# Folding v into w_in: the low parts as eight 64-row products that share one round

## The chip, the cores and the metric

One Trainium2 chip, one of its cores. The metric is the device time of one execution in microseconds (us). The matrix engine is called PE here (its weight loads PEld), the vector engine DVE, the scalar engine ACT, GpSimd POOL; SP issues most transfers.

## The reference

Eight batches of eight heads; 576 tokens, head size 64, 32 memory slots per head. The attention is followed by a feed-forward layer.

```python
a = softmax(phi over the 32 slots)                     # (b, h, s, m)
k_m = einsum('bhsm,bhsd->bhmd', a, k)                  # 32 x 64 per head
v_m = einsum('bhsm,bhsd->bhmd', a, v)
attn = softmax(q @ k_m.T / 8)                          # 576 x 32 per head
x = concat over heads of (attn @ v_m)                  # 4608 x 512
h = x @ w_in                                           # 4608 x 2048
out = (h * cos(h)) @ w_out                             # 4608 x 512
```

## The kernel before

`x` is never formed. For each batch the kernel folds `v_m` into `w_in`: for head h the 32 x 64 block of `v_m` times the 64 rows of `w_in` that belong to it gives 32 rows of a table `vw`, 256 rows (8 heads) by 2048 columns for a batch. The first product of the feed-forward layer is then `vw` times the attention weights (`gemm1`, L568), the second one multiplies by `w_out` (`gemm2`, L628). Both have float16 operands in two parts, a high one and a low one (what the float16 rounding left over), as three products: high by high, high by low, low by high.

The main loop runs over 12 groups of 384 tokens and, in a group, over 16 steps f of 128 columns of `h`. A step is `gemm1` (six matmuls of 384 columns into a PSUM tile `hp`), then sine and products on ACT and DVE (`act`, `act_end`: L593, L598, L603, L607, L609, L610), which leave the tile `gp`, and, four steps later (LAG), `gemm2` (nine matmuls of 512 columns into three `acc` tiles). Between them stand the preparation of the next batch (`memory`: maximum and exponential of phi, L304 and L310, the sums `psA` of L256, the turned sums `tpx`, from which `spread_k` fills `km` and `spread_v` fills `vm`; then `attend`: the scores `sc` of L401, their softmax, and `aT`) and its fold.

The fold of a batch goes by quarters q of 512 columns, and in a quarter by halves g of four heads (128 rows of `vw`); half and half stand in one step of the loop, the quarters four steps apart. `fold_psum` writes a half into a PSUM tile `pv`, a whole bank; `split_fold` then makes the high part on ACT (L505) and the low one on DVE (L507). `pv` comes out of a pool of two banks (`ps_s`), which `sc`, `psA`, `tpx` and others share. For the batches 0 and 1 the fold is in float32 (L492). From batch 2 on (`b >= 2`) `v` too has a high part `vp` and a low part `vl`, made in `scales` (L368 to L370), and `w2` holds for each head pair c and head o of it the high part of `w_in` in that head's own 64 partitions and the low part in the 64 partitions of the other. A product of `vp` over all 128 rows is so high by high plus high by low. `vl` is filled in the head's own 64 rows and zero in the others, so that its product over 128 rows is low by high. A product is 32 columns of weights wide and goes to 32 partitions of `pv`; four of them, j = 0 to 3, one for each head, stand side by side. I call four such matmuls of 512 columns, one beside the other, a round.

Up to the middle of the first groups the order is written out by hand (`ORDER`); from the loop on, a scheduler decides the order of each engine's instructions out of the program's order and its own estimate.

Of the kernel before, what the change touches and what calls it, by code (L numbers as in the profile page):

```python
# [20 lines left out]
P = 128  # L21
B, H, S, D, M = 8, 8, 576, 64, 32
# [3 lines left out]
NP = H // 2  # L26
# [47 lines left out]
def attention_then_ffn(ctx: ExitStack, tc: tile.TileContext, phi, phiT, kv, kv_first, qT, w_in, w_out, eye, out):  # L74
    nc = tc.nc
# [8 lines left out]
    def small_ps(name):  # L84
        return ps_s.tile([P, 512], F32, tag="ps_s", name=name)
# [16 lines left out]
    vl = const.tile([P, NP, 2, M], F16, name="vl")  # L102
    nc.vector.memset(vl, 0.0)

    loads, st = {}, {}
# [87 lines left out]
    def to_range(name, pool, tag, e):  # L193
        t = pool.tile([P, 1], F32, tag=tag, name=name)
        nc.vector.reciprocal(out=t, in_=e)
        nc.vector.tensor_scalar(out=t, in0=t, scalar1=2.0 ** 14, scalar2=None, op0=ALU.mult)
        return t
# [62 lines left out]
    def blank(b):  # L260
        st["km", b] = wk.tile([P, NP, 2 * M], F32, tag="km", name=f"km_{b}", bufs=1)
        st["vm", b] = wk.tile([P, NP, 2 * M], F32, tag="vm", name=f"vm_{b}")
        nc.gpsimd.memset(st["km", b], 0.0)
        nc.gpsimd.memset(st["vm", b], 0.0)

    def spread_k(b, tpx):
        tv = tpx[:, 0:HM].rearrange("p (c t m) -> p c t m", t=2, m=M)
        nc.scalar.mul(st["km", b][0:D, :, 0:M], tv[0:D, :, 0], 1.0 / math.sqrt(D))
        nc.scalar.mul(st["km", b][D:P, :, M:2 * M], tv[D:P, :, 1], 1.0 / math.sqrt(D))

    def copier(name):
        return nc.scalar.copy if name in COPY_ACT else nc.vector.tensor_copy

    def spread_v(b, tpx, copy):
        tv = tpx[:, 0:HM].rearrange("p (c t m) -> p c t m", t=2, m=M)
        copy(out=st["vm", b][D:P, :, 0:M], in_=tv[D:P, :, 0])
        copy(out=st["vm", b][0:D, :, M:2 * M], in_=tv[0:D, :, 1])

    def bound(b, X):
        l1 = wk.tile([P, 4], F32, tag="l1", name=f"l1_{b}")  # L280
# [7 lines left out]
    def memory(b):  # L288
# [42 lines left out]
        for g in range(2):  # L331
            nc.tensor.transpose(tpx[:, g * P:(g + 1) * P], X[:, g], ident)
        blank(b)
        spread_k(b, tpx)
        spread_v(b, tpx, nc.vector.tensor_copy)
        yield
        l2 = bound(b, X)
# [12 lines left out]
    def scales(b):  # L350
        E = wk.tile([P, 1], F32, tag="E", name=f"E_{b}", bufs=3)
        nc.vector.tensor_scalar(out=E, in0=st["ev", b], scalar1=st["e", "in"], scalar2=None, op0=ALU.mult)
        cu = wk.tile([P, 1], F32, tag="cu", name=f"cu_{b}", bufs=3)
        nc.vector.tensor_scalar(out=cu, in0=E, scalar1=2.0 ** -27 / (2.0 * math.pi), scalar2=None, op0=ALU.mult)
        st["E", b], st["cu", b] = E, cu
        if b < 2:
            T = wk.tile([P, 1], F32, tag="T", name=f"T_{b}")
            nc.vector.reciprocal(out=T, in_=E)
            nc.vector.tensor_scalar(out=T, in0=T, scalar1=2.0 ** 13, scalar2=None, op0=ALU.mult)
            st["T", b] = T  # L360
        else:

            sv = to_range(f"sv_{b}", wk, "sv", st["ev", b])
            vp = wk.tile([P, NP, 2, M], F16, tag="vp", name=f"vp_{b}", bufs=1)
            for o in range(2):
                here, there = slice(o * D, (o + 1) * D), slice((1 - o) * D, (2 - o) * D)
                vm = st["vm", b][here, :, (1 - o) * M:(2 - o) * M]
                nc.scalar.activation(vp[here, :, o], vm, AF.Copy, scale=sv[here])  # L368
                nc.scalar.activation(vp[there, :, o], vm, AF.Copy, scale=sv[here])
                nc.vector.scalar_tensor_tensor(out=vl[here, :, o], in0=vm, scalar=sv[here], in1=vp[here, :, o],  # L370
                                               op0=ALU.mult, op1=ALU.subtract)
            st["vp", b] = vp
# [114 lines left out]
    def fold_psum(b, q, g):  # L487
        pv = small_ps(f"pv_{b}_{q}_{g}")
        for i in range(2):
            c = 2 * g + i  # L490
            if b < 2:
                nc.tensor.matmul(pv[D * i:D * (i + 1)], lhsT=st["vm", b][:, c],  # L492
                                 rhs=w_in_sb[:, 2 * q:2 * q + 2, c], start=True, stop=True)
        if b >= 2:
            for first in (True, False):
                for j in range(4):
                    c, o = 2 * g + j // 2, 1 - j % 2
                    nc.tensor.matmul(pv[M * j:M * (j + 1)], lhsT=(st["vp", b] if first else vl)[:, c, o],  # L498
                                     rhs=st["w2", q][:, c, o], start=first, stop=not first, skip_group_check=True)
        return pv  # L500

    def split_half(b, vw, g, src, part):
        T = st["T", b] if b < 2 else 2.0 ** -15
        if part == 0:
            nc.scalar.activation(vw[:, 0, g], src, AF.Copy, scale=T)  # L505
        else:
            nc.vector.scalar_tensor_tensor(out=vw[:, 1, g], in0=src, scalar=T, in1=vw[:, 0, g],  # L507
                                           op0=ALU.mult, op1=ALU.subtract)

    def split_fold(b, vw, g, src):  # L510
        for part in range(2):
            split_half(b, vw, g, src, part)

    def fold(b, q, g):
        if g == 0:
            st["vw", b, q] = wk.tile([P, 2, 2, FS], F16, tag="vw", name=f"vw_{b}_{q}", bufs=8)
        split_fold(b, st["vw", b, q], g, fold_psum(b, q, g))

    def fold_first(j, x=slice(0, WS)):
        pv = small_ps(f"pvf_{j}").rearrange("p (g x) -> p g x", g=2)  # L520
# [326 lines left out]
    for v, k in enumerate("kv"):  # L847
# [3 lines left out]
        put(f"X{k}0_1", lambda: norm(0, 1))  # L851
        put(f"tp{k}0", lambda: turn_x(0))
    put("blank0", lambda: blank(0))
    put("km0", lambda: spread_k(0, r["tpk0"]))
    put("vm0", lambda: spread_v(0, r["tpv0"], copier("vm0")))

    def after_memory(b):
        if b:
            for c in range(5):
                put(f"ga{b}_{c}", lambda c=c: gathered(b, c))  # L860
            put("den1", lambda: den_of(1))
            put(f"X{b}_0", lambda: norm(b, 0))
            put(f"X{b}_1", lambda: norm(b, 1))
            put(f"tpx{b}", lambda: turn_x(b))
            put(f"blank{b}", lambda: blank(b))
            put(f"km{b}", lambda: spread_k(b, r[f"tpx{b}"]))
            put(f"vm{b}", lambda: spread_v(b, r[f"tpx{b}"], copier(f"vm{b}")))
        put(f"bound{b}", lambda: set_bound(b))
        put(f"acr{b}", lambda: turn_column(st["l2", b], b))
        put(f"level{b}", lambda: level(b))  # L870
        put(f"att{b}", lambda: do.setdefault(b, attention(b)))
# [39 lines left out]
    for kind, j in blocks:  # L911
# [5 lines left out]
        for w, tag in halves:  # L917
# [10 lines left out]
            if kind == "in":  # L928
                x = slice(0, WS) if w is None else slice(w * P, (w + 1) * P)
# [87 lines left out]
    for b in range(2):  # L1017
        put(f"sc_{b}", lambda b=b: scales(b))
    for g in range(2):
        for part, engine in enumerate(("ACT", "DVE")):  # L1020
            put(f"hi0_{g}_{part}", lambda g=g, part=part: scaled(0, 0, g, st["vf", 0][:, g], part))
        put(f"fo1_{g}", lambda g=g: fold_psum(1, 0, g))
        for part, engine in enumerate(("ACT", "DVE")):
            put(f"hi1_{g}_{part}", lambda g=g, part=part: scaled(1, 0, g, r[f"fo1_{g}"], part))
# [41 lines left out]
    for i in range(NF, 12 * NF):  # L1066
# [21 lines left out]
        for b, q, g in folds.get(i, ()):  # L1088
            if q == g == 0:
                scales(b)  # L1090
            fold(b, q, g)
# [70 lines left out]
```

## Time and profile before

| | us |
|---|---|
| time, median of 3 runs (lowest, highest) | 692.75 (692.67, 693.51) |
| the profiled execution's own time | 693.0 |
| its span, first to last instruction | 691.2 |

Busy time in the span of 691.2 us: PE 680.5, DVE 528.0, ACT 502.9, POOL 36.6, weight loads 360.7. Busy times of PE count each matmul from its start to its modelled end, and these overlap; the distance from the start of one to the start of the next tells more. The chain that ended last is a walk back from the last instruction to what released it; what stands on it is where time can be gained or lost. Verdicts below go by the median.

### The profile page before, as it was taken

What the parts mean: (1) busy time and instruction counts of PE and PEld (TensorE: products, weight loads), DVE (VectorE), ACT (ScalarE), POOL (GpSimd) and SP (SyncE); (2) the same over time, 40 slices, a digit from 0 to 9 for tenths busy, and PEclk for the clock granted to TensorE, in tenths of its full rate; (3) what the DMA queues carried; (4) which work ended last, traced back from release to release, by engine and by line L of the source; (5) the groups of instructions that cost most, each with busy time, mean ns of one, the idle gap of its engine ahead of it and who ended that gap; (6) DMA issues with size and microseconds to landing.
All of it is one profiled execution on the core that took longest, in us unless ns stands there. A gap on an engine that the chain in (4) does not pass through costs nothing.

```text
span 691.2 us, 12016 instructions
## 1 busy us (share of the span) xinstructions
PE 680.5 (98%) x4670; PEld 360.7 (52%) x4670; DVE 528.0 (76%) x1125; ACT 502.9 (73%) x950; POOL 36.6 (5%) x51
## 2 busy tenths in 40 slices
PE   8999999999999999999999999999999999999997
PEld 4545455564544446655454445655445445565553
DVE  6878889999989965798668876599667886566552
ACT  3677878998987866887776965878667875665652
POOL 3433100000001000010000000010000000000000
PEclk9999999999999999999999999999999999999999
DMA  8998906038246100430105300250100100100101
GB/s 300 393 353 328 347 12 176 1 78 271 61 151 153 46 0 25 168 97 1 46 3 172 114 1 2 71 184 34 47 1 1 46 1 1 46 1 1 46 1 46
DMA packets 32585, 66.17 MB, mean 96 GB/s; under 512 B 2192, under 2 KB 12496, under 8 KB 32528
## 3 DMA queue, kind: packets, MB, share of 16 engines
q1 hardware_dynamic: 28208, 57.55, 25.6%
q10 hardware_dynamic: 4320, 7.87, 3.0%
q8 instruction: 36, 0.59, 0.3%
q14 instruction: 21, 0.17, 0.1%
HBM read 51.77 MB, written 9.44 MB: 89 GB/s over the span
## 4 chain that ended last, share of the span: by engine, by line
PE 79%; ACT 10%; DVE 7%; DMA 2%; issue 1%; SPq 0%
PE acc L628 40%; PE hp L568 21%; PE acc L623 6%; PE pv L498 3%; PE hp L559 2%; PE sc L401 2%; ACT u L603 2%; ACT gp L593 2%; ACT L414 1%; DMA raw_in<-in_w_in 1%; PE psA L256 1%; ACT L603 1%; DVE gp L610 1%; PE pv L492 1%; PE warm L666 1%
## 5 line engine op out<-in xcount | busy, mean ns | idle before, releaser
L628 PE MATMUL acc<-wo,gp 128*128 128x512 f16 x1584 | 370.9, 379 | 0.1
L628 PEld LDWEIGHTS <-gp 128*128 128x128 f16 x1584 | 153.7, 98 | 161.5 <-issue 1.2
L568 PE MATMUL hp<-aT,vw 128*128 128x192 f16 (+1 forms) x1440 | 203.4, 284 | 0.8 <-DVE u L607 0.6
L568 PEld LDWEIGHTS <-vw 128*128 128x128 f16 x1440 | 127.1, 98 | 79.7 <-issue 20.0
L603 ACT ACTIVATE u<-u,quarter 128x384 f32<-128x384 f32 x176 | 107.1, 614 | 68.1 <-DVE u L598 65.5
L607 DVE SCALAR_TENSOR_TENSOR u<-hp,u 128x384 f32<-128x384 f32 x176 | 96.5, 553 | 61.4 <-ACT u L603 61.0
L598 DVE SCALAR_TENSOR_TENSOR u<-hp,cu,gp 128x192 f32<-128x192 f32 (+1 forms) x240 | 115.8, 503 | 21.6 <-ACT gp L593 20.3
L610 DVE TENSOR_TENSOR gp<-u,gp 128x384 f16<-128x384 f32 x176 | 97.0, 553 | 39.3 <-ACT gp L609 37.8
L593 ACT ACTIVATE gp<-hp,cu 128x192 int32<-128x192 f32 (+1 forms) x240 | 111.0, 489 | 18.1 <-PE hp L568 14.2
L609 ACT CAST gp<-u 128x384 f16<-128x384 f32 x176 | 89.0, 508 | 48.1 <-DVE u L607 47.5
L623 PE MATMUL acc<-wo,gp 128*128 128x512 f32 x96 | 44.3, 597 | 0.2 <-DVE wo L182 0.2
L507 DVE SCALAR_TENSOR_TENSOR vw<-pv,vw 128x512 f16<-128x512 f32 x48 | 31.8, 684 | 2.2 <-ACT vw L505 2.1
L505 ACT ACTIVATE vw<-pv 128x512 f16<-128x512 f32 x48 | 26.9, 589 | 4.8 <-PE pv L498 4.7
L623 PEld LDWEIGHTS acc<-wo,gp 128*128 128x128 f32 x96 | 17.5, 190 | 19.4 <-issue 15.9
L644 ACT ACTIVATE ob<-acc,os 128x512 f32<-128x512 f32 x28 | 18.5, 683 | 11.4 <-PE acc L628 8.8
L603 ACT ACT_TABLE_LOAD x19 | 24.4, 1283 | 0.3
L401 PE MATMUL sc<-q,km 128*64 128x256 f32 (+3 forms) x192 | 20.0, 335 | 0.6 <-issue 0.5
L414 ACT ACT_TABLE_LOAD x15 | 19.2, 1283 | 0.3
L559 PE MATMUL hp<-aT,vf 128*128 128x384 f32 x52 | 19.2, 492 | 0.0
L256 PE MATMUL psA<-kv,phi 128*32 128x129 f32 (+1 forms) x560 | 18.0, 275 | 0.1
L339 POOL PARTITION_ALL_REDUCE l<-l x6 | 2.5, 414 | 285.8 <-DVE l L285 273.1
L401 PEld LDWEIGHTS sc<-q,km 128*64 128x64 f32 x192 | 11.3, 136 | 11.5 <-issue 6.2
(167 smaller groups left out, 557.0 us busy)
## 6 DMA issues: line engine op xcount, KB each, us to landing
kv<-in_kv SPq DMA_DIRECT2D x28, 516.0 KB, 7.2
raw_out<-in_w_out SPq DMA_DIRECT2D x8, 1024.0 KB, 9.7
q<-in_qT SPq DMA_DIRECT2D x7, 1152.0 KB, 5.6
out<-ob ACTq DMA_DIRECT2D x30, 256.0 KB, 2.1
raw_in<-in_w_in SPq DMA_DIRECT2D x5, 1024.0 KB, 11.6
phi<-in_phi SPq DMA_DIRECT2D x7, 512.0 KB, 6.0
w_in_sb<-w_in_parts SPq DMA_DIRECT2D x12, 256.0 KB, 4.5
phiT<-in_phiT SPq DMA_DIRECT2D x4, 576.0 KB, 5.7
```

The source lines that it names most:

```text
L401: nc.tensor.matmul(sc[D * p:D * (p + 1), g * n:(g + 1) * n], lhsT=km[:, 2 * g + p], rhs=qt[:, 2 * g + p, t0:t0 + n], start=True, stop=True)
L507: nc.vector.scalar_tensor_tensor(out=vw[:, 1, g], in0=src, scalar=T, in1=vw[:, 0, g], op0=ALU.mult, op1=ALU.subtract)
L559: nc.tensor.matmul(hp[:, :GT], lhsT=st["vf", q][:, g, fo * P:(fo + 1) * P], rhs=st["aTf"][:, g], start=(g == 0), stop=(g == 1))
L568: nc.tensor.matmul(hp[:, c0:c0 + n], lhsT=vw[:, wi, g, fo * P:(fo + 1) * P], rhs=aT[:, ai, g, c1:c1 + n], start=(k == 0), stop=(k == 5))
L593: ins = nc.scalar.activation(ni[:, c0:c0 + n], hp[:, c0:c0 + n], AF.Copy, scale=turns, bias=0.25)
L598: nc.vector.scalar_tensor_tensor(out=u[:, c0:c0 + n], in0=hp[:, c0:c0 + n], scalar=turns, in1=ni[:, c0:c0 + n], op0=ALU.mult, op1=ALU.subt ...
L603: nc.scalar.activation(u, u, AF.Sin, scale=TWO_PI_BELOW, bias=quarter)
L607: nc.vector.scalar_tensor_tensor(out=u, in0=hp[:, :GT], scalar=2.0 ** -17, in1=u, op0=ALU.mult, op1=ALU.mult)
L609: nc.scalar.copy(gp[:, 0], u)
L610: nc.vector.tensor_tensor(out=gp[:, 1], in0=u, in1=gp[:, 0], op=ALU.subtract)
L623: nc.tensor.matmul(accs[grp][t], lhsT=gp[:, t * P:(t + 1) * P], rhs=wo[:, f + 1], start=(f == 0), stop=(f == NF - 1))
L628: nc.tensor.matmul(accs[grp][t], lhsT=gp[:, gi, t * P:(t + 1) * P], rhs=parts[:, wi], start=(f == 0 and gi == 0 and wi == 0), stop=(f == N ...
```

## The change

The low parts are multiplied over the head's own 64 rows alone, without the rows of zeros, and those of both halves together: eight products, each of 64 rows by 32 columns, two of them (one of each half, on different rows) above one another in the same 32 columns of the engine. So that the two never want the same 64 rows, half 1 takes its two heads of a pair in the other order (`spot`); `spread_k` and `spread_v` follow that order, and `spread_k` has four small instructions for two. `vm` is packed into 32 columns and needs no zeros any more. `split_fold` of both halves comes after the low products of both.

```diff
-        nc.gpsimd.memset(st["vm", b], 0.0)
+        if b < 2:
+            nc.gpsimd.memset(st["vm", b], 0.0)
...
-        nc.scalar.mul(st["km", b][0:D, :, 0:M], tv[0:D, :, 0], 1.0 / math.sqrt(D))
-        nc.scalar.mul(st["km", b][D:P, :, M:2 * M], tv[D:P, :, 1], 1.0 / math.sqrt(D))
+        for cs, turned in (((slice(0, NP), 0),) if b < 2 else ((slice(0, 2), 0), (slice(2, NP), 1))):
+            for t in range(2):
+                rows, x = slice(t * D, (t + 1) * D), t ^ turned
+                nc.scalar.mul(st["km", b][rows, cs, x * M:(x + 1) * M], tv[rows, cs, t], 1.0 / math.sqrt(D))
...
         if b >= 2:
-            for first in (True, False):
-                for j in range(4):
-                    c, o = 2 * g + j // 2, 1 - j % 2
-                    nc.tensor.matmul(pv[M * j:M * (j + 1)], lhsT=(st["vp", b] if first else vl)[:, c, o],
-                                     rhs=st["w2", q][:, c, o], start=first, stop=not first, skip_group_check=True)
+            for j in range(4):
+                c, o = spot(g, j)
+                nc.tensor.matmul(pv[M * j:M * (j + 1)], lhsT=st["vp", b][:, c, o], rhs=st["w2", q][:, c, o],
+                                 start=True, stop=False, skip_group_check=True)
         return pv
+
+    def spot(g, j):
+        return 2 * g + j // 2, 1 - j % 2 if g == 0 else j % 2
+
+    def fold_low(q, pvs):
+        for j in range(4):
+            for g in range(2):
+                c, o = spot(g, j)
+                rows = slice(o * D, (o + 1) * D)
+                nc.tensor.matmul(pvs[g][M * j:M * (j + 1)], lhsT=vl[rows, c, o], rhs=st["w2", q][rows, c, o],
+                                 start=False, stop=True, skip_group_check=True)
...
-        split_fold(b, st["vw", b, q], g, fold_psum(b, q, g))
+        if b < 2:
+            split_fold(b, st["vw", b, q], g, fold_psum(b, q, g))
+            return
+        st["pv", g] = fold_psum(b, q, g)
+        if g == 1:
+            fold_low(q, [st["pv", 0], st["pv", 1]])
+            for x in range(2):
+                split_fold(b, st["vw", b, q], x, st["pv", x])
```

The scheduler orders the instructions anew. There are 24 quarters with `b >= 2` (six batches of four). On PE, quarter 1 of batch 3 stood like this before (the number behind a name tells one tile from another; `vp_2615` is batch 3's, `vl` is one tile for all):

```order
L628 MATMUL acc_2_2412<-wo,gp_10_2592 128x512
L498 LDWEIGHTS vp_2615
L498 MATMUL pv_1_0_2742<-w_in_sb,vp_2615 32x512
...
L498 LDWEIGHTS vl
L498 MATMUL pv_1_0_2742<-w_in_sb,vl 32x512
...
L498 LDWEIGHTS vp_2615
L498 MATMUL pv_1_1_2753<-w_in_sb,vp_2615 32x512
...
L498 LDWEIGHTS vl
L498 MATMUL pv_1_1_2753<-w_in_sb,vl 32x512
...
L568 LDWEIGHTS vw_3_2507
```

Each pair of rows stands four times there. Now, with the changed file's line numbers (L502 the high products, L515 the low ones; the first two pairs stand four times, and the last two take turns until each stood four times):

```order
L651 MATMUL acc_2_2414<-wo,gp_10_2594 128x512
L502 LDWEIGHTS vp_2617
L502 MATMUL pv_1_0_2744<-w_in_sb,vp_2617 32x512
...
L502 LDWEIGHTS vp_2617
L502 MATMUL pv_1_1_2749<-w_in_sb,vp_2617 32x512
...
L515 LDWEIGHTS vl
L515 MATMUL pv_1_0_2744<-w_in_sb,vl 32x512
L515 LDWEIGHTS vl
L515 MATMUL pv_1_1_2749<-w_in_sb,vl 32x512
...
L591 LDWEIGHTS vw_3_2509
```

What moved: four groups of four became two groups of four and one of eight. 19 quarters go from the first form to the second like this one. Five do not. Quarter 0 of batch 2 stood in three pieces with `gemm1` and `gemm2` between them and now stands in one piece, some thirty matmuls later in the order. In quarter 1 of batch 2 one low matmul now stands ahead of the second half's high ones and the other seven behind them. Quarter 0 of batch 5 stood in two pieces (nine and seven matmuls) and still does (two groups of high ones and one low matmul, then 66 others, then seven low ones). In quarter 3 of the batches 3 and 5 both halves stand apart as before. Batch 3's quarter 3 before, on PE:

```order
L498 MATMUL pv_3_0_3093<-w_in_sb,vp_2615 32x512
...
L498 LDWEIGHTS vl
L498 MATMUL pv_3_0_3093<-w_in_sb,vl 32x512
...
L628 LDWEIGHTS gp_3_2939
```

and now:

```order
L502 MATMUL pv_3_0_3095<-w_in_sb,vp_2617 32x512
...
L515 LDWEIGHTS vl
L515 MATMUL pv_3_0_3095<-w_in_sb,vl 32x512
...
L651 LDWEIGHTS gp_3_2941
```

Here nothing moved; the four low matmuls (four in each half) are 64-row ones now.

On ACT the order moved around batch 2's `vp` and batch 3's exponential (`phi_1592`, L310 before and L315 now). An ACT_TABLE_LOAD stands where ACT goes from the sine of L603 (L626 now) to the exponential or back. Before:

```order
L609 CAST gp_9_1905<-u_9_1904 128x384
L442 ACTIVATE aT_1684<-back_512_1921 128x2x64
L224 ACTIVATE w_in_parts_1866<-w_in_sb,s_in 128x512
L603 ACTIVATE u_10_1934<-u_10_1934,quarter 128x384
L310 ACT_TABLE_LOAD
L310 ACTIVATE phi_1592<-phi_1592 128x1024
L609 CAST gp_10_1935<-u_10_1934 128x384
L310 ACTIVATE phi_1592<-phi_1592 64x256
L603 ACT_TABLE_LOAD
L603 ACTIVATE u_11_1967<-u_11_1967,quarter 128x384
```

Now:

```order
L315 ACT_TABLE_LOAD
L315 ACTIVATE phi_1592<-phi_1592 128x1024
L632 CAST gp_7_1843<-u_7_1842 128x384
L626 ACT_TABLE_LOAD
L626 ACTIVATE u_8_1877<-u_8_1877,quarter 128x384
...
L315 ACT_TABLE_LOAD
L315 ACTIVATE phi_1592<-phi_1592 64x256
L632 CAST gp_9_1906<-u_9_1905 128x384
L626 ACT_TABLE_LOAD
L626 ACTIVATE u_10_1935<-u_10_1935,quarter 128x384
```

The exponential moved three steps ahead and its two instructions stand apart, with a pair of table loads around each: two loads more, 46 for 44 in the program. Batch 2's four `vp` instructions, which stood among steps 6 to 9, now stand behind step 10's sine. On PE the scores `sc` of batch 2's first block, four matmuls in a row before, stand two and two now, with two `gemm1` matmuls between them.

## Rows read from the trace of the kernel before

**Rows 1.** The page's first part (busy time, share of the span, instructions) and, of its second part, PE's granted clock in 40 slices of the span (9 is 90% of full speed or more).

```profile
PE 680.5 (98%) x4670; PEld 360.7 (52%) x4670; DVE 528.0 (76%) x1125; ACT 502.9 (73%) x950; POOL 36.6 (5%) x51
PEclk9999999999999999999999999999999999999999
```

**Rows 2.** Who waited for whom, PE alone, from 186 us to the end: engine, line, what it waited for, us in total, times, longest.

```profile
PE pv L498 <- DVE vw L507: 0.6, 2, 0.3
PE sc L401 <- issue: 0.4, 1, 0.4
PE pv L498 <- DVE phi L304: 0.3, 1, 0.3
```

**Rows 3.** The page's fourth part: the chain that ended last, by engine.

```profile
PE 79%; ACT 10%; DVE 7%; DMA 2%; issue 1%; SPq 0%
```

**Rows 4.** Busy time by stretch (us from the span's start; length, then busy us and instructions of each engine, granted clock, DMA share, GB/s).

```profile
180.00:190.00 10.00, 10.00 (x58) 5.06 (x55) 9.28 (x19) 9.72 (x22) 0.00 (x0) 1.00 0.45 106
190.00:200.00 10.00, 9.69 (x120) 5.01 (x123) 8.67 (x17) 9.38 (x16) 0.31 (x1) 1.00 0.05 12
```

**Rows 5.** PE in order of time around one quarter (batch 3, quarter 0): start, us from the first start to the last end of the group, line, operation, rows*columns of the engine used, shape, count.

```profile
243.33 1.67 PE L628 MATMUL acc<-wo,gp 128*128 128x512 f16 x7
244.94 0.40 PE L498 MATMUL pv<-w_in,vp 128*32 128x512 f16 x4
245.16 0.39 PE L498 MATMUL pv<-w_in,vl 128*32 128x512 f16 x4
245.38 0.39 PE L498 MATMUL pv<-w_in,vp 128*32 128x512 f16 x4
245.60 0.39 PE L498 MATMUL pv<-w_in,vl 128*32 128x512 f16 x4
245.92 1.15 PE L568 MATMUL hp<-aT,vw 128*128 128x384 f16 x6
246.90 2.11 PE L628 MATMUL acc<-wo,gp 128*128 128x512 f16 x9
248.85 0.33 PE L568 MATMUL hp<-aT,vw 128*128 128x384 f16 x1
```

**Rows 6.** The sums `psA` of batch 3 (float32, 129 columns, four side by side; the last token chunk has 64 rows). PE's order of time, asked in short windows from 199.75 to 200.26, each of which begins with another round; the start is what is read.

```profile
199.56 0.29 PE L256 MATMUL psA<-kv,phi 128*32 128x129 f32 x4
199.78 0.31 PE L256 MATMUL psA<-kv,phi 64*32 64x129 f32 x4
199.92 0.50 PE L256 MATMUL psA<-kv,phi 64*32 64x129 f32 x11
200.03 0.40 PE L256 MATMUL psA<-kv,phi 64*32 64x129 f32 x8
```

**Rows 7.** PE in order of time around batch 2's quarter 0; [idle before <- what ended it].

```profile
187.95 2.10 PE L628 MATMUL acc<-wo,gp 128*128 128x512 f16 x9
189.99 0.40 PE L498 MATMUL pv<-w_in,vp 128*32 128x512 f16 x4
190.32 1.15 PE L568 MATMUL hp<-aT,vw 128*128 128x384 f16 x6
191.30 1.46 PE L628 MATMUL acc<-wo,gp 128*128 128x512 f16 x6
193.07 0.40 PE L498 MATMUL pv<-w_in,vp 128*32 128x512 f16 x4 [0.31 <-DVE phi L304]
193.41 0.82 PE L628 MATMUL acc<-wo,gp 128*128 128x512 f16 x3
...
194.32 0.61 PE L498 MATMUL pv<-w_in,vl 128*32 128x512 f16 x8
194.87 0.99 PE L568 MATMUL hp<-aT,vw 128*128 128x384 f16 x5
195.69 2.10 PE L628 MATMUL acc<-wo,gp 128*128 128x512 f16 x9
```

**Rows 8.** ACT in order of time, same stretch.

```profile
189.09 0.51 ACT L609 CAST gp<-u 128x384 f16<-128x384 f32 x1 [0.16 <-DVE u L607]
190.94 1.28 ACT L310 ACT_TABLE_LOAD   x1
192.24 1.06 ACT L310 ACTIVATE phi<-phi 128x1024 f32<-128x1024 f32 x1
...
193.60 0.41 ACT L310 ACTIVATE phi<-phi 64x256 f32<-64x256 f32 x1
194.03 1.28 ACT L603 ACT_TABLE_LOAD   x1
```

**Rows 9.** DVE's last work on `gp` (steps 9 and 10), and what `vw` and `vp` cost: the two rows of time, then rows of the tile `pv` and of line 368 (count, ns least/median/most, first and last start).

```profile
189.69 0.55 DVE L610 TENSOR_TENSOR gp<-u,gp 128x384 f16<-128x384 f32 x1
194.20 0.56 DVE L610 TENSOR_TENSOR gp<-u,gp 128x384 f16<-128x384 f32 x1
L505 ACT ACTIVATE vw<-pv x48: 577/589/600, 195.8 to 604.8; 128x512 f16<-128x512 f32 x48
L507 DVE SCALAR_TENSOR_TENSOR vw<-pv,vw x48: 651/683/692, 196.5 to 606.3; 128x512 f16<-128x512 f32 x48
L368 ACT ACTIVATE vp<-vm,sv x12: 384/396/409, 183.1 to 534.4; 64x128 f16<-64x128 f32 x12
```

More of the change, by code (lines that the diff above doesn't have):

```diff
@@ L275, in spread_v @@
         tv = tpx[:, 0:HM].rearrange("p (c t m) -> p c t m", t=2, m=M)
-        copy(out=st["vm", b][D:P, :, 0:M], in_=tv[D:P, :, 0])
-        copy(out=st["vm", b][0:D, :, M:2 * M], in_=tv[0:D, :, 1])
+        for t in range(2):
+            rows, x = slice((1 - t) * D, (2 - t) * D), t if b < 2 else 0
+            copy(out=st["vm", b][rows, :, x * M:(x + 1) * M], in_=tv[rows, :, t])
     def bound(b, X):
@@ L366, in scales @@
                 here, there = slice(o * D, (o + 1) * D), slice((1 - o) * D, (2 - o) * D)
-                vm = st["vm", b][here, :, (1 - o) * M:(2 - o) * M]
+                vm = st["vm", b][here, :, 0:M]
                 nc.scalar.activation(vp[here, :, o], vm, AF.Copy, scale=sv[here])
```

## The prediction

> **What bounds the kernel now.** I read the busy times first. PE is busy for 680.5 of 691.2 us at full granted clock throughout [rows 1], but those times overlap, so I asked what PE waited for. From 186 us on the list holds waits of 0.3 to 0.4 us that come to about 2 us in all; those that this change touches are in [rows 2]. The chain that ended last stands on PE for 79% of the span [rows 3]. So PE's own list of work sets the end, and a matmul round that goes away is gained, unless PE then waits. The second thing to see is how near the other engines are where the order moved. Between 180 and 200 us ACT is busy 9.72 and 9.38 of 10 us and DVE 9.28 and 8.67 [rows 4]: there is little room there for more work on ACT.
>
> **What a quarter costs on PE, before and after.** Nine `gemm2` matmuls take from 246.90 to 248.85, 0.216 each [rows 5]: 512 columns at the full clock. The last seven before the quarter begin at 243.33, so the next matmul was due at 243.33 + 7 x 0.216 = 244.84. The first round of four begins at 244.94, the others 0.22 apart, and the next `gemm1` at 245.92 [rows 5]. So the quarter takes 1.08 us: four rounds of 0.216, 0.10 to go from 128*128 to 128*32 and 0.10 (0.32 less 0.216) to go back, 0.01 left over. The four of a round begin almost together: the group of four lasts 0.40 where one matmul lasts 0.39.
>
> Now there are three rounds, the last with eight matmuls, and one more change of form, from 128*32 to 64*32. That change is in the trace once per batch, in float32: rounds of `psA` follow at 0.11 (199.92 to 200.03); across the change it is 0.22 (199.56 to 199.78), and the round after it comes 0.14 later [rows 6]. So it costs 0.11 + 0.03 = 0.14 there, and the changes of the float16 rounds above cost 0.10. I take 0.12, with 0.10 and 0.14 as ends. Four more starts in the last round are 0.01. A quarter of the plain kind then saves 0.216 - 0.12 - 0.01 = 0.08 us, and 19 of them 1.6 us.
>
> This holds if all eight products run beside each other. No row of before shows two products above one another in the same columns. The bounds are nothing (one round of 0.216) and a second round (0.216 more per quarter). I take the lower bound, because four side by side cost no more than one [rows 5], the two halves use different rows of the engine and different banks, and each 64 rows feed four products just as now.
>
> From the last round's start to the next `gemm1` the rows have 0.32, where a matmul of that round is recorded for 0.39 [rows 5]: the next form begins before the recorded end. The Trainium skill has a rule here that speaks against the change: TensorEngine Tiling (Array Packing), section Key Properties, says that changing the tiling mode, and not just the tile, drains the engine. If a drain lasts until the recorded end, the sum below would come to +0.2 us for the forecast's -0.8 (the last rival, worked out there from rows); the trace agrees that a change costs time, and shows less of it.
>
> **The other five quarters and the moved instructions.**
>
> Quarter 0 of batch 2 took three pieces: 189.90 (187.95 + 9 x 0.216) to 190.32, 0.42; 192.60 (191.30 + 6 x 0.216) to 193.41, 0.81 with the wait of 0.31; and 0.55 from 194.32 to 194.87 with 0.10 in front [rows 7]. That is 1.88, and in one piece it is 1.08 - 0.08 = 1.0: 0.9 saved.
>
> Quarter 1 of batch 2 has its lone low matmul between the high ones: a round of its own and three changes more than before, four rounds as before, so 3 x 0.12 = 0.36 more. The scores behind it waited 0.4 for a bank [rows 2]; now they stand one `gemm2` matmul later and behind both splits, which I take to cover that wait. Together nothing.
>
> Quarter 3 of the batches 3 and 5 keeps its four rounds and gets two changes more, 0.24 each. Its second half waits 0.3 for a bank now [rows 2], and the delay in front of it hides there: 0.3 for both. Quarter 0 of batch 5 loses a round (five become four) and gets one change: 0.1 saved.
>
> The scores of batch 2 in two pieces: two more changes at 0.10 and a `km` that is ready later for the second pair: 0.3 lost, between 0.2 and 0.5.
>
> Batch 3's exponential with two more table loads, 1.28 each [rows 8], is the one place where ACT can hold PE up. The cast of step 9 began at 189.09 [rows 8] and `gp` was ready at 189.69 + 0.55 = 190.24, when PE wanted it at 195.69 [rows 7, 9]: 5.4 us to spare. In the new order three loads (3.84) and both exponentials (0.96 and 0.4 by their distances) stand ahead of that cast, and the four `vp` (0.40 each [rows 9]) and one conversion (about 0.5) behind it: 189.09 + 5.2 - 2.1 = 192.2, a good 193.4 for `gp`. PE meanwhile comes earlier, because the three fold pieces (1.88) and one `gemm1` (0.98, from 245.92 to 246.90 [rows 5]) now stand behind: 195.69 - 2.9 + 0.3 = 193.1. So it waits about 0.3 there, and the second pair of loads, the `vp` behind step 10 and the low products that need them come after that. Bounds: 0, if what PE has left to do covers it, and 2.6, both loads. I take 1.2, near the middle.
>
> At nothing I put four edits. The `vm` memsets go, on POOL, which nobody waits for. `spread_k` has two instructions more per batch, at most 0.4 each by the nearest row [rows 9], while `sc` follows some matmul steps later; on batch 2 it is in the 0.3 above. The first half's split starts one round and a change later, 0.59 on ACT and 0.68 on DVE a half [rows 9]; its reader stands at least five loop steps, some 14 us, further on, and only where a bank of the pool is wanted at once does it show (the waits above). The exit from 64*32 back to 128*128 I price like that from 128*32.
>
> **Sum.** -1.6 - 0.9 + 0 + 0.3 - 0.1 + 0.3 + 1.2 = -0.8 us. The profiled execution took 693.0 us (span 691.2, 1.8 around it), which makes 692.2; the median of the runs is 0.25 below the profiled one, so on it I predict 692.0. A measurement of this kernel tells about 0.2%, 1.4 us, from no change.
>
> **Rivals.**
>
> The pairs above one another don't overlap (slower). If the second product of each 32 columns waits for the first, the low products take two rounds again, and the change of form comes on top. That is 0.216 more in 22 quarters (all but the two that stand apart), 4.8 us: -0.8 + 4.8 = +4.0, 696.8. It decides from 0.04 us on: when the shared round takes over 0.25 instead of 0.216, the gain is gone. For it speaks that no row shows such a pair; against it, that side by side costs nothing.
>
> PE never waits for ACT at 195 (faster). Then term seven is nothing, and with a change of form at 0.10 the 19 quarters save 0.4 more: -0.8 - 1.2 - 0.4 = -2.4, 690.4. For it speak the 5.4 us that `gp` had to spare; against it the sum for step 9.
>
> ACT's two loads land on PE in full, and a change of form is 0.14: -0.8 + 1.4 + 0.4 = +1.0, 693.8. ACT's 97% between 180 and 190 speaks for it.
>
> Each change of form waits for the recorded end of the last matmul. Then the new change costs 0.39 - 0.216 = 0.17, a plain quarter saves 0.03, and 19 of them lose 1.0 of the 1.6: +0.2, 693.0. The 0.32 in [rows 5] and the 0.22 in [rows 6] (against 0.29, as long as the round before it lasted) speak against it. By the rule of the Trainium skill named above (TensorEngine Tiling (Array Packing), Key Properties), read strictly, this would be the case.
>
> **Chances and range.** Forecast (-2.0 to +0.5 around -0.8) 0.55; no wait for ACT 0.19; loads in full 0.10; pairs in turn 0.11; full drain 0.05. Faster by over 0.2% (below 691.4) are the second case and a seventh of the first: 0.27. Slower (above 694.1) are the pairs in turn, half of the loads in full with something on top: 0.16. Within 0.2%: 0.57. The range goes from 690.4 (no wait) to 694.4 and leaves the pairs in turn and a little below out. The likeliest case alone reaches from 690.8 to 693.3.
>
> **What would show it.** In a plain quarter: three groups of `pv` 0.22 apart up to the second, then about 0.33 from the second to the third, one group of eight lasting about 0.41, and 0.32 to the next `gemm1`; 1.00 us where 1.08 was. If the group of eight lasts about 0.6, the pairs take turns. Batch 2's quarter 0 in one piece. Between 180 and 205 us four table loads on ACT for two, and PE idle for about 1.2 us behind `gp`, `vp` or `vl`; no idle time there, or over 2 us, would make the sum wrong by as much. From 330 us on the distance to before should grow by 0.08 per quarter and by nothing else.

## The result, and the profile after

The changed kernel takes 696.63 us (median of 5 runs, 695.40 to 697.97) where the kernel before took 692.75: 1.0053 times as long, with a 95% interval of 1.0035 to 1.0070. It is slower by about 0.5%, above the predicted range. The profiled execution took 695.46 us with a span of 693.7, the second fastest of the five; its span is 2.5 us longer than that of before. So the trace below accounts for 2.5 of the 3.9 us between the medians (for 2.9 of 3.3 where the change was measured again), and the rest is in no trace.

The page of after (busy times and granted clock as in [rows 1], the chain as in [rows 3]):

```profile
PE 680.2 (98%) x4670; PEld 358.4 (52%) x4670; DVE 527.3 (76%) x1125; ACT 507.4 (73%) x964; POOL 33.3 (5%) x45
PEclk9999999999999999999999999999999999999999
...
PE 65%; ACT 17%; DVE 10%; DMA 4%; issue 2%; POOL 0%; SPq 0%; ACTq 0%; POOLq 0%
```

The granted clock is full throughout (a mean of 1.00), and PE has as many matmuls as before and 0.3 us less busy time, but the chain that ended last has moved: PE's share fell from 79% to 65%, and ACT's rose from 10% to 17%. So PE now waits. For whom, from 186 us on, the list of PE's waits of after says (compare [rows 2], whose kernel had about 2 us in all):

```profile
PE hp L591 <- DVE u L630: 1.9, 4, 0.6
PE sc L406 <- DVE vw L523: 1.0, 1, 1.0
PE acc L651 <- ACT gp L632: 0.6, 1, 0.6
PE pv L502 <- ACT vp L374: 0.5, 1, 0.5
PE acc L651 <- ACT ob L667: 0.3, 1, 0.3
PE pv L502 <- DVE vw L523: 0.3, 2, 0.2
PE tpx L337 <- DVE X L332: 0.3, 1, 0.3
```

The shared round itself does what it should. The plain quarter of [rows 5] in after, PE in order of time:

```profile
245.29 1.67 PE L651 MATMUL acc<-wo,gp 128*128 128x512 f16 x7
246.89 0.62 PE L502 MATMUL pv<-w_in,vp 128*32 128x512 f16 x8
247.44 0.41 PE L515 MATMUL pv<-w_in,vl 64*32 64x512 f16 x8
247.78 1.15 PE L591 MATMUL hp<-aT,vw 128*128 128x384 f16 x6
```

Eight products of 64 rows take 0.41 us from the first start to the last end, where four of 128 rows took 0.39 or 0.40 [rows 5]. From the time that the quarter was due (245.29 + 7 x 0.216 = 246.80) to the next `gemm1` are 0.98 us, where 1.08 was.

Where the time went shows when the same `gemm2` matmul (the same by count) is set beside that of before. The next table gives how far its distance to the profiled execution of before grows in each stretch of the span, for after and for the runs of the next section. It begins at 160 us, because ahead of that one profile differs from another by up to 1.0 us either way (column "ahead"), with the same kernel too: transfers at the start.

```
us          160-230 230-310 310-330 330-363 363-388 388-520 520-545 545-680   sum | ahead
after         +2.50   +0.24   +0.21   -0.18   -0.29   -0.15   +0.96   -0.32 +2.96 | -0.46
after again   +2.12   +0.25   +0.21   -0.18   -0.34   -0.15   +0.95   -0.33 +2.52 | +0.38
km4           +3.54   +0.01   +0.30   +0.00   -0.13   +0.31   +0.00   +0.00 +4.03 | -0.80
low128        +2.89   +0.00   +0.29   +0.00   +0.78   +0.29   +0.49   +0.00 +4.74 | +0.09
km2           -0.08   +0.89   -0.09   -0.18   +0.80   -0.44   +0.62   -0.30 +1.21 | -0.62
scores        -0.08   +0.89   -0.09   -0.18   +1.15   -0.44   +0.34   -0.30 +1.27 | +0.38
plain         +0.09   +0.00   -0.10   -0.18   +0.83   -0.55   +0.34   -0.31 +0.12 | -0.85
packed        +0.01   +0.00   -0.00   +0.00   +0.39   +0.00   +0.00   -0.00 +0.40 | +0.69
none          +0.10   +0.00   -0.00   +0.00   -0.23   -0.00   -0.00   -0.00 -0.13 | -0.83
nine          +0.10   -0.02   -0.00   +0.00   -0.12   -0.18   +0.00   -0.32 -0.54 | -1.01
thirteen      -0.11   -0.19   -0.09   -0.09   -0.01   -0.36   +0.00   -0.31 -1.16 | +0.33
fourteen      -0.11   -0.01   -0.09   -0.09   +0.51   -0.36   +0.00   -0.31 -0.45 | -0.74
```

Each plain quarter takes 0.09 off. Two places put more on: the stretch from 160 to 230 us, around batch 2's fold, and the place at 534 us, behind batch 6's last quarter. The first, PE in order of time in after:

```profile
192.24 1.14 PE L591 MATMUL hp<-aT,vw 128*128 128x384 f16 x6
193.98 2.12 PE L651 MATMUL acc<-wo,gp 128*128 128x512 f16 x9 [0.61 <-ACT gp L632]
196.50 1.14 PE L591 MATMUL hp<-aT,vw 128*128 128x384 f16 x6 [0.40 <-DVE u L630]
197.47 1.03 PE L651 MATMUL acc<-wo,gp 128*128 128x512 f16 x4
198.97 0.61 PE L502 MATMUL pv<-w_in,vp 128*32 128x512 f16 x8 [0.48 <-ACT vp L374]
```

And ACT there (in [rows 8] the whole exponential of `phi` stands behind one load):

```profile
191.81 1.28 ACT L315 ACT_TABLE_LOAD   x1
193.11 0.42 ACT L315 ACTIVATE phi<-phi 64x256 f32<-64x256 f32 x1
193.43 0.49 ACT L632 CAST gp<-u 128x384 f16<-128x384 f32 x1
193.94 1.28 ACT L626 ACT_TABLE_LOAD   x1
195.24 0.61 ACT L626 ACTIVATE u<-u,quarter 128x384 f32<-128x384 f32 x1
...
196.22 0.39 ACT L373 ACTIVATE vp<-vm,sv 64x128 f16<-64x128 f32 x1
```

The cast for `gemm2` ends at 193.92 and PE starts at 193.98; the activation behind the second load ends at 195.85, DVE's `u` follows, and PE starts at 196.50; `vp` comes last. One chain on ACT, and PE waits at three of its links. A row of waiting is less than what it costs: it counts from the recorded end of a matmul, 0.38 after its start, where the next could have started at 0.216, so each such wait costs PE some 0.16 more. Counted from start to start, over what the round or the change of form takes without a wait, PE lost 3.07 us between 162 and 230 us in after and 0.83 in before.

The second place, PE, then ACT, then DVE:

```profile
533.48 0.41 PE L515 MATMUL pv<-w_in_sb,vl 64*32 64x512 f16 x8
533.82 1.64 PE L591 MATMUL hp<-aT,vw 128*128 128x384 f16 x9
536.46 1.08 PE L406 MATMUL sc<-q,km 128*64 128x256 f32 x8 [1.01 <-DVE vw L523]
```

```profile
534.18 0.51 ACT L632 CAST gp<-u 128x384 f16<-128x384 f32 x1 [0.65 <-DVE u L630]
534.60 0.40 ACT L373 ACTIVATE vp<-vm,sv 64x128 f16<-64x128 f32 x1
534.90 1.05 ACT L521 ACTIVATE vw<-pv 128x512 f16<-128x512 f32 x2
```

```profile
535.51 1.29 DVE L523 SCALAR_TENSOR_TENSOR vw<-pv,vw 128x512 f16<-128x512 f32 x2
```

The scores want a bank of the small pool. Both are held by the quarter's halves until the shared round has ended at 533.89, and then ACT first casts `gp` and writes a `vp`, because the splits stand behind those in its list. In before the first half's split stood ahead of that cast, and that profile has no wait there:

```profile
531.73 0.60 ACT L505 ACTIVATE vw<-pv 128x512 f16<-128x512 f32 x1 [0.42 <-PE pv L498]
532.22 0.50 ACT L609 CAST gp<-u 128x384 f16<-128x384 f32 x1
```

### The profile page after: what moved, and what is told of

It is laid out like the page before. It is cut to its first block, busy times and chain, and to the rows that moved or that the text cites. A ratio compares the mean times of both kernels' runs of the same rounds, so it can differ in the third digit from the quotient of the medians.

```text
span 693.7 us, 12027 instructions
## 1 busy us (share of the span) xinstructions
PE 680.2 (98%) x4670; PEld 358.4 (52%) x4670; DVE 527.3 (76%) x1125; ACT 507.4 (73%) x964; POOL 33.3 (5%) x45
## 4 chain that ended last, share of the span: by engine, by line
PE 65%; ACT 17%; DVE 10%; DMA 4%; issue 2%; POOL 0%; SPq 0%; ACTq 0%; POOLq 0%
PE acc L651 34%; PE hp L591 18%; PE acc L646 5%; DMA raw_out<-in_w_out 4%; ACT u L626 3%; ACT gp L616 2%; ACT gp L632 2%; DVE gp L633 2%; DVE u L630 2%; DVE u L621 2%; ACT L419 2%; ACT L626 2%; PE sc L406 1%; PE pv L502 1%; PE hp L582 1%
## 5 line engine op out<-in xcount | busy, mean ns | idle before, releaser
L626 ACT ACTIVATE u<-u,quarter 128x384 f32<-128x384 f32 x176 | 107.1, 614 | 64.7 <-DVE u L621 62.1
```

The source lines that it names most:

```text
L626: nc.scalar.activation(u, u, AF.Sin, scale=TWO_PI_BELOW, bias=quarter)
```

## The experiments

**What the order costs, and what the shared round gives.** Four kernels on one chip.

The kernel before with `spread_k` alone as changed, but not turned (`km4`):

```
-        nc.scalar.mul(st["km", b][0:D, :, 0:M], tv[0:D, :, 0], 1.0 / math.sqrt(D))
-        nc.scalar.mul(st["km", b][D:P, :, M:2 * M], tv[D:P, :, 1], 1.0 / math.sqrt(D))
+        for cs in ((slice(0, NP),) if b < 2 else (slice(0, 2), slice(2, NP))):
+            for t in range(2):
+                rows = slice(t * D, (t + 1) * D)
+                nc.scalar.mul(st["km", b][rows, cs, t * M:(t + 1) * M], tv[rows, cs, t], 1.0 / math.sqrt(D))
```

> The kernel before, with one edit of the change: ScalarE writes km of batches 2 and later in four instructions of two column pairs instead of two of four; the layout of km, vm and the fold are those of before. Theory A (what the change lost between 185 and 225 us comes from the order in which the scheduler then puts ScalarE's and PE's work around the first plain fold, and the four km instructions alone set that order): 46 table loads instead of 44, PE idle right after 193 us and in the 205 us stretch as in the changed kernel, and 1.5 to 2.2 us over before, 694.2 to 695.0. Theory B (the loss comes from the fold itself: both banks held until the shared round has ended, and matmuls of 64 rows): 692.5 to 693.0, no difference from before but for two short instructions.

696.22 us, ratio 1.0048 (1.0035 to 1.0061): nearly all that the whole change lost, with the old fold. Its waits on PE from 186 us on:

```profile
PE hp L570 <- DVE u L609: 1.9, 4, 0.6
PE sc L403 <- POOL l L341: 0.7, 1, 0.7
PE acc L630 <- ACT gp L611: 0.6, 1, 0.6
...
PE pv L500 <- ACT vp L371: 0.5, 1, 0.5
```

Five of its waits stand where after has them and are as long to 0.07 us (at 189, 194, 196.5, 199 and 206.7 us). That of the scores for POOL's `l`, at 212 us, is not in after's first profile, and its second one has 0.27 of it. The trace has 46 table loads, as after has, for the 44 of before. Theory A held, and the price was larger than it said: +3.54 between 160 and 230 us, and 0.30 twice more (behind 314 and 476 us), both of which after has too. Theory B fell.

The changed kernel with two `km` instructions (`km2`): the tile is 320 columns wide, and a step of 160 and 96 columns puts the turned pairs where the change wants them.

```
+                x = 3 if t else 5
+                dst = st["kmw", b][rows, t * M:t * M + 2 * x * M].rearrange("p (a i m) -> p a i m", a=2, m=M)
+                dst = dst[:, :, 0:3:2]
+                src = tv[rows, :, t].rearrange("p (a i) m -> p a i m", a=2)
+            nc.scalar.mul(dst, src, 1.0 / math.sqrt(D))
```

> The changed kernel, with km of batches 2 and later written by two ScalarE instructions through a wider tile, so that the turned columns come out without the split; the fold with its shared round of 64-row products is that of the change. Theory A (the order that the four km instructions set): 44 table loads, the waits between 185 and 225 us as before, and what is left is the shared rounds' saving (19 plain quarters by about 0.09 = -1.7) against the waits that later banks cost (1.0 at the quarter before batch 7's scores, two times 0.3 elsewhere): 692.2 to 693.0. Theory B (the fold itself): as the changed kernel, 695.4 to 697.0.

693.78 us, ratio 1.0016 (1.0007 to 1.0025). The loss between 160 and 230 us is gone and the trace has 44 table loads, as A said, but the time lies above A's range. The shared rounds' 1.7 us are more than given back, at more places than after had shown: 0.89 net between 230 and 310 us (among it one product of a quarter that slips forward alone, with its changes of form, and a wait of 0.35 behind ACT's copy at 276), 0.80 around 375, 0.62 around 534. Its longest waits ("issue" says that the profile shows nothing that PE waited for; whether it is a bank is tested next):

```profile
PE sc L413 <- issue: 1.6, 2, 1.0
PE sc L413 <- DVE vw L530: 0.7, 1, 0.7
```

The changed kernel with low products over 128 rows, half by half (`low128`; the loops over g and j in `fold_low` also change places):

```
-                nc.tensor.matmul(..., lhsT=vl[rows, c, o], rhs=st["w2", q][rows, c, o], ...)
+                nc.tensor.matmul(..., lhsT=vl[:, c, o], rhs=st["w2", q][:, c, o], ...)
```

> The changed kernel, with the low products over 128 rows (the zeros of the spread stand in the rows that the change leaves out) and half by half, four and four, behind both halves' high rounds; the order of work, the km in four instructions and the packed vm stay as in the change. Theory A (the shared round saves, the order loses): each of some 22 quarters takes 0.09 us more on PE or more, since an eight becomes two fours: 2 us over the changed kernel, 697.4 to 699. Theory B (the 64-row form itself costs time somewhere): as the changed kernel or faster, 694.5 to 696.6.

697.03 us, ratio 1.0055 (1.0041 to 1.0069). The medians can't part it from after (696.63 and, below, 696.00). The table does: in the quarters where after gains 0.09 each it gains nothing (330 to 363 and 545 to 680 us: 0.00 for -0.18 and -0.32). So the gain is that of the shared round of 64-row products. The time lies between A's range and B's; that the 64-row form costs nothing elsewhere this run can't show by itself, since other orders moved with it (+0.78 between 363 and 388 us, +0.49 at 534).

The kernel before with `vm` packed and without its memset (`packed`):

> The kernel before, with only vm packed: from batch 2 on vm holds no zeros, its memset on GpSimd is gone and the scaling of v reads it from the first columns. Both theories: 692.4 to 693.1, the same as before. A difference of more than 0.5 us would say that the memset's place on GpSimd counts, which the prediction set at nothing.

693.48 us, ratio 1.0007 (0.9997 to 1.0016). The median lies above the expected range, 0.53 over before's 692.95 on that chip, which is just past the 0.5 that the expectation named as a sign; the interval includes no change. The 0.40 that its profile has more all arises around 375 us, behind a transfer (last section), and ACT, DVE and PE have the order of before. `none`, below, has no such memsets either and shows no difference.

**Is it the hold of the banks?** In `km2`, the two quarters ahead of scores fold half by half again (`scores`), or all quarters but sixteen do (`plain`); and the change once more.

```
+        if (b, q) in BY_HALF:
+            for j in range(4):
+                c, o = spot(g, j)
+                nc.tensor.matmul(st["pv", g][M * j:M * (j + 1)], lhsT=vl[:, c, o], rhs=st["w2", q][:, c, o],
+                                 start=False, stop=True, skip_group_check=True)
+            split_fold(b, st["vw", b, q], g, st["pv", g])
+            return
```

> The kernel of the run with km in two instructions and the shared round, in which two quarters alone, the last ones of batches 4 and 6, which stand right ahead of the next batch's scores, fold half by half as before: each half's low products over 128 rows behind its high ones, and its bank free for its split at once. Theory A (a shared round keeps both banks of the small pool and the two splits of a quarter until it has ended, and where scores want a bank at once PE waits for it): the waits of the scores at 374.6 us (0.99) and 534.5 us (0.67) are gone, two savings of 0.09 with them, about 1.5 us less than that run: 692.0 to 692.6. Theory B (those waits come from elsewhere, from ScalarE or VectorE being late in any case): the waits stay, 693.5 to 694.0.

> As the run with km in two instructions, but the shared round is kept only for the quarters whose four rounds stand together and that no scores follow (16 of 24); all of batch 2 and the last quarters of batches 3 to 6 fold half by half with 128 rows. Theory A: the waits of the scores are gone, the stretch up to 240 us is that of the kernel before, and each of the plain quarters gives 0.09 us: 16 by 0.09 = 1.4 us under the kernel before, 691.3 to 691.9, unless the wait of 0.35 us at 276 us (PE behind ScalarE's copy of a result out of PSUM) comes from the shared round of batch 3's third quarter, and then 691.7 to 692.2. Theory B (the saving is given back at other waits wherever the shared round stands): 692.6 to 693.6.

> The changed kernel once more, beside the others on one chip: 695.4 to 697.0. Its trace should show the same waits as the first one at 194, 196.5, 199, 313, 474 and 536 us to 0.05 us, if they come from the order of the instructions; waits that move between the two executions come from transfers or from chance.

`scores`: 693.61 us, 1.0016 (1.0006 to 1.0025), no gain on `km2`. The wait of the scores at 374.6 is gone, and one of 1.20 stands at 389, PE behind ACT's `ob`. At 534 the wait fell from 0.67 to 0.30. So with the hold of the banks the scores' wait goes, but at 375 it cost next to nothing by itself (about 0.1 us, by the measure of the next part): DVE and ACT were late in any case. A named the wait and was wrong on its price. `plain`: 693.29 us, 1.0006 (0.9997 to 1.0015), by the time B. The change again: 696.00 us, 1.0050 (1.0037 to 1.0064), with the waits at the same places, most to 0.02 us; one of 0.24 at 189 is missing, that at 194 is 0.45 for 0.61, and one of 0.27 at 212 is new. The order sets most of them.

**Why the kernels with two `km` instructions lose the saving at 388 us.** In `plain`, DVE in order of time, then PE:

```profile
375.12 0.33 DVE L382 SCALAR_TENSOR_TENSOR vl<-vm,sv,vp 64x128 f16<-64x128 f32 x1
375.75 0.35 DVE L382 SCALAR_TENSOR_TENSOR vl<-vm,sv,vp 64x128 f16<-64x128 f32 x1 [0.29 <-ACT vp L380]
376.13 0.72 DVE L419 STREAM_TRANSPOSE at<-sc 128x512 f32<-128x512 f32 x1
...
377.95 0.61 DVE L637 SCALAR_TENSOR_TENSOR u<-hp,cu,gp 128x384 f32<-128x384 f32 x1
```

```profile
386.77 1.46 PE L667 MATMUL acc<-wo,gp 128*128 128x512 f16 x6 [0.92 <-ACT ob L683]
```

The second `vl` stands ahead of the scores' transposition and waits 0.29 there for ACT. In the kernel before it comes behind:

```profile
376.15 0.70 DVE L407 STREAM_TRANSPOSE at<-sc 128x512 f32<-128x512 f32 x1
...
378.15 0.61 DVE L598 SCALAR_TENSOR_TENSOR u<-hp,cu,gp 128x384 f32<-128x384 f32 x1
...
379.39 0.35 DVE L370 SCALAR_TENSOR_TENSOR vl<-vm,sv,vp 64x128 f16<-64x128 f32 x1
```

A load that DVE waits for ahead of this moves the whole stretch too (last section), so the order's own price is read from DVE's `mx` behind that load (369.49 in before) to the `u` of these rows: 8.66 or 8.67 us in before and in all runs with one `vl` ahead but the change itself (`packed`, `km4`, and `none`, `nine`, `thirteen` and `fourteen` below), 9.60 in `plain` and `scores` and 9.71 in `km2`, which have both ahead. The order costs 0.94 there, whatever the load does. The changed kernel has one `vl` ahead like before, and 7.73:

```profile
377.90 0.33 DVE L375 SCALAR_TENSOR_TENSOR vl<-vm,sv,vp 64x128 f16<-64x128 f32 x1
378.16 0.70 DVE L412 STREAM_TRANSPOSE at<-sc 128x512 f32<-128x512 f32 x1
```

So this loss is no part of what the change lost (its stretch from 363 to 388 us is 0.29 shorter than before's). Two kernels test the order: `none` has `km2`'s layout and no shared round, so that PE, ACT and DVE have the order of before, and `nine` has shared rounds in nine quarters that leave that order alone but for the first halves' splits (`BY_HALF` has the others).

> Packed vm, the second half's columns turned and km in two instructions as in the run with two km instructions, but no shared round at all: every half folds its high and its low products by itself over 128 rows. The instructions stand in the order of the kernel before on every engine. Theory A (order and shared rounds are all that counts): 692.4 to 693.0, no difference from before. If the turned columns or the wider km tile cost something by themselves: over 693.3.

> As the run without shared rounds, with shared rounds in nine quarters: the first three of batch 3, the second and third of batch 5 and the four of batch 7. With these nine ScalarE's and VectorE's instructions keep the order of before but for the first half's split, which falls behind one or two others. Theory A' (a saving of 0.09 stays where the order of the other engines stays; what the sixteen shared quarters gave back at 388 us came from VectorE's second piece of vl standing ahead of the scores' transposition): no new wait at 388 us, 9 by 0.092 = 0.83 us under the kernel without shared rounds, less about 0.1 at 276 us: 691.8 to 692.2. Theory B' (VectorE and ScalarE bound the stretch round 385 us whatever their order, so savings ahead of it are lost): only batch 5's and 7's six quarters count, 0.55 us under: 692.1 to 692.5, and PE's wait at 388 us grows by what batch 3 saved, 0.2 to 0.3 us.

`none`: 692.52 us, ratio 1.0000 (0.9991 to 1.0009). Turned columns, the wider tile and the packed `vm` cost nothing that shows. `nine`: 692.41 us, 0.9992 (0.9984 to 1.0001), by the time B', but without the wait at 388 that B' expected. DVE there:

```profile
374.85 0.34 DVE L382 SCALAR_TENSOR_TENSOR vl<-vm,sv,vp 64x128 f16<-64x128 f32 x1
375.11 0.70 DVE L419 STREAM_TRANSPOSE at<-sc 128x512 f32<-128x512 f32 x1
...
377.11 0.60 DVE L637 SCALAR_TENSOR_TENSOR u<-hp,cu,gp 128x384 f32<-128x384 f32 x1
```

0.26 from `vl` to the transposition, where `plain` has 1.01, and `u` is 0.84 earlier (0.68 without what the two profiles differ by ahead of 160 us). A' held for the place and not for the time; batch 3's three savings (0.28) were still lost, at 275 and 287 us.

It is the third quarters of batches 4 and 6, the last shared ones ahead of scores, that move DVE's order. Without them thirteen quarters can share, and fourteen with batch 3's third:

> As the run with nine shared quarters, with thirteen: batch 2's first, the first two of batches 3, 4 and 6, the second and third of batch 5 and the four of batch 7. The third quarters of batches 4 and 6, which make VectorE put both pieces of vl ahead of the scores' transposition, fold by halves; the order on ScalarE and VectorE is that of before but for the first half's splits and one conversion. Theory A': 12 plain quarters by 0.092 and 0.2 of batch 2's first = 1.3 us under the kernel without shared rounds: 691.1 to 691.6, and no PE wait over 0.1 at 388 or 534 us. Theory B' (ScalarE and VectorE bound batch 5's and 7's scores whatever their order): 692.0 to 692.4 with waits of 0.3 and more at those two places.

> The same with the third quarter of batch 3 shared as well. If that quarter's later splits are what made PE wait 0.1 us for ScalarE's copy out of PSUM at 275 us and 0.16 at the next quarter, it gives nothing: within 0.2 us of the run with thirteen. If its saving of 0.09 stays, 0.1 us under it; a median can't tell these two, so the trace decides: the distance to before at 290 us.

`thirteen`: 691.61 us, 0.9985 (0.9976 to 0.9993): faster than both kernels, than before by 1.1 us at the medians, the upper end of what A' expected. Its waits on PE from 210 us on are those of before:

```profile
PE hp L607 <- DVE u L646: 0.6, 2, 0.3
PE pv L509 <- DVE vw L532: 0.5, 2, 0.3
```

`fourteen`: 691.99 us, 0.9985 (0.9977 to 0.9994). Between 230 and 310 us it gains 0.01 where `thirteen` gains 0.19: batch 3's third quarter loses what it and the two before it gave. At the medians it is 0.38 above `thirteen`, where 0.2 at most was expected; its profile has 0.51 between 363 and 388 us, with DVE in the order of before, from the load of the last section.

## Why the prediction was wrong, point by point

- **The shared round: right.** Predicted 1.00 us for a plain quarter, measured 0.98; the steps were 0.33 predicted and 0.32 measured from the second high round (247.51 - 0.39 = 247.12) to the shared one. The change of form costs 0.12 as assumed (0.98 less three rounds of 0.216, two changes of 0.10 and 0.01). The rival of pairs in turn fell with the group of eight, 0.41. So did the full drain: a change at the recorded end would put 0.39 between those starts. The Trainium skill's rule (TensorEngine Tiling (Array Packing), Key Properties) is that a change of mode drains the engine. The trace agrees in that a change costs, 0.10 to 0.12 us; how long a drain lasts the page does not say, and to the recorded end it does not last here.
- **"Bounds: 0 ... and 2.6, both loads. I take 1.2": the step that failed.** For the stretch up to 230 us the terms made +0.6 (-0.9 + 0 + 0.3 + 1.2); it came to +2.1 and +2.5, and in `km4`, without the shared round's gains, to +3.5. The place was right: `gp` was to be ready at 193.4 and was at 193.9. But the term priced PE's wait for `gp` once. PE waited at four more places (for `u` at 189 and 196 us, `vp` and `X`), and each cost some 0.16 more than its row shows: in after the five come to 2.8 us from start to start (0.40, 0.77, 0.56, 0.55 and 0.48), where the term had 1.2 and its upper bound 2.6. The upper bound counted the loads, and not the `vp` that ACT put behind them.
- **The cause of that order was put at nothing.** "`spread_k` has two instructions more per batch" was priced as 0.8 us of ACT at most. `km4` and `km2` show that these two set the new order of batch 3's exponential and of `vp`. The prediction took the moved order as it stood and did not ask which edit had moved it.
- **"Only where a bank of the pool is wanted at once does it show": half right, and priced at nothing.** It shows at 534 us (+0.96). The later split has a second effect that the step did not see: other instructions on ACT and DVE pass it. At 534 us these are ACT's cast and a `vp`; in the kernels with two `km` instructions a `vl` also came ahead of the scores at 375 us (0.94 in `plain`), which the change itself was spared.
- **"From 330 us on the distance should grow by 0.08 per quarter and by nothing else"** fails at 474 (0.30) and 534 us, and between 363 and 388 us, where one quarter stands and 0.29 was gained.
- **What the sum missed.** With 2.8 for 1.2 it would come to +0.8. Of the rest up to the +2.96 of the table, 0.96 stands at 534 us, 0.6 at 314 and 476 us, and some 0.4 between 230 and 310 us, where +0.24 was measured and the terms made about -0.2: PE waits 0.34 there behind ACT's copy at 278 us.
- **Memsets: right, as far as the runs tell.** `none` has ratio 1.0000 without them, and the interval of `packed` includes no change.

What stays open: why two more short instructions change the scheduler's list so much was not tried, and the 0.3 at 316 and 476 us are known only to come with the four `km` instructions.

## What to carry to other kernels

When a change shortens PE's list, read the order of the engines that feed it before pricing anything else: here 1.7 us of PE work were really saved (19 quarters by 0.09), two more instructions of 0.2 us per batch reordered ACT for 3.5 us, and a result that came two rounds later let other work pass ahead of it. Where a chain on another engine is reordered, price each link at which PE takes from it, not only the first, and add what a row of waiting leaves out. A saving was kept where the order around it stayed and no later split delayed what PE waits for: thirteen quarters gained 1.1 us, a fourteenth in the same order took back what its batch had gained, and all twenty-two, with the order that came with the change, lost 3.9 and, the second time, 3.3.

## What the runs showed of the hardware

- Eight matmuls of 64 rows by 32 columns, two above one another in each 32 columns and into two banks, last 0.41 us as a group, as long as four of 128 rows (0.40): the pairs run fully beside each other.
- One transfer sets the stretch from 365 to 388 us. DVE's maximum over `phi` stands ahead of `gemm1`'s `u` in its list and waits for a load that took 5.5 to 6.4 us from issue to landing from one kernel's profile to another's. In before, in `packed` and in `fourteen`:

```profile
369.49 0.69 DVE L244 TENSOR_TENSOR mx<-phi 128x512 f32<-128x512 f32 x1 [1.29 <-DMA phi<-in_phi]
```

```profile
370.58 0.69 DVE L244 TENSOR_TENSOR mx<-phi 128x512 f32<-128x512 f32 x1 [1.68 <-DMA phi<-in_phi]
```

```profile
368.96 0.69 DVE L244 TENSOR_TENSOR mx<-phi 128x512 f32<-128x512 f32 x1 [1.79 <-DMA phi<-in_phi]
```

Less the time ahead of 160 us, `packed` is 0.40 later there (370.58 - 0.69 - 369.49) and 0.40 later at 388; `fourteen` is 0.21 later (368.96 + 0.74 - 369.49) and stands at +0.21 by 388 (its sums up to there), though PE had come 0.30 earlier. `packed` has the order of before on PE, ACT and DVE, so the order of these engines does not explain its 0.40. I take it for chance of one execution, as large as four shared rounds; that is not shown, since the one kernel with two profiles, the change, has 6.4 and 6.3 us for this load.
